# A transformer block on one core: the turned differences of the down weights pass through three buffers, the first square root goes first, and the order is another

## The chip, the cores and the metric

The kernel runs on one core of a Trainium2 chip. The metric is the device time of one execution in microseconds (us). Five engines work on it side by side, each through its own list of instructions in a fixed order: PE (TensorE, matrix products; PEld is its loading of weights), DVE (VectorE), ACT (ScalarE), POOL (GpSimd) and SP (SyncE, which here issues nearly all DMAs). An engine that reaches an instruction whose inputs aren't there yet waits, and everything behind that instruction in its list waits with it.

## The reference

One layer on 2048 rows of 640 numbers, in fp32: layer norm, windowed attention with 32 heads in which a row looks at 8 rows with a distance of 2 between them, a projection, a second layer norm, and a gated feed-forward part of width 1728.

```python
def _A_ref(x, wqkv, wo):                 # H = 32, Dh = 20, W = 8, dil = 2
    qkv = (x @ wqkv).reshape(B, S, 3, H, Dh)
    ...
    logits = jnp.einsum("bhsd,bhswd->bhsw", q, kg) * scale
    attn = _softmax(jnp.where(mask[None, None, :, :], logits, -1e9), axis=-1)
    o = jnp.einsum("bhsw,bhswd->bhsd", attn, vg)
    return o.transpose(0, 2, 1, 3).reshape(B, S, D) @ wo

def _B_ref(x, w_gate, w_up, w_down):
    return (_silu(x @ w_gate) * (x @ w_up)) @ w_down

h = x + _A_ref(_layernorm(x), A_wqkv, A_wo)
h2 = h + _B_ref(_layernorm(h), B_w_gate, B_w_up, B_w_down)
```

## The kernel before, in words

**Rows and numbers.** The 2048 rows are worked on in four blocks (0 to 3) of 512 rows, each as four groups of 128 rows. A product of two fp32 matrices is made of products of split numbers: each operand is cut into a high part (a cast to fp32r, on ACT) and the rest (a subtraction on DVE), and PE multiplies high by high, high by low and low by high. So ahead of most operands stand an ACT cast and a DVE subtraction.

**Stages.** First come the layer norms and the products with `wqkv` (L664), while DVE does the attention (L703 to L790) group by group up to about 564 us. The projection (`wo`, L911), the second layer norm and the feed-forward part follow block by block: `ffn(b)` for blocks 0 and 1 (L983, L994), and for blocks 2 and 3 a scheme in which products of sums and differences of the two blocks and of halves of the weights are combined. From that scheme come `early` (L1067, L1114), the ends of blocks 2 and 3 (L1089, L1124), `pair` (L1067 with L1208 to L1268) and `down_products` (L1315).

**The turned differences.** `down_combinations(p)`, for p = 0 to 5, loads two pieces of the down weights (L1141), makes four differences of them on DVE (L1144), and then twice, for h = 0 and 1: a copy to fp32r on ACT (L1147), the rest on DVE (L1148), and a store of both into the DRAM buffer `tsc` (L1150, 640 KB each). `down_products` reads them back at L1328. All twelve stores leave from one place of the tile `acts`, columns 2048 to 3328. A copy at L1147 therefore can't begin before the store ahead of it has read that place out.

**Start.** A dummy square root at L366 brings ACT's table of square roots in. The first 128 rows are loaded first (L593); `one_split` works on them on ACT (L442, a sum over columns 384 to 639) and on DVE (L446 to L450, the mean and its subtraction). Then come PE's transposes (L625), the casts (L627) and the rest (L628). Ten products of zeros (L575, `warm`) run on PE while the rows are on their way.

**What sets the order.** Every step is added to a planner `Plan` with its engine, a guessed cost, and what it reads and writes. The planner lists all 2846 steps by due times, and then moves single steps by a table `SHIFT` (step number: us) before it writes them out. `P.add` finds what a step must wait for from its reads and writes, so a new buffer gives other waits by itself.

**Names.** `fa` and `ra` are the large fp32 and fp32r tiles, `bank` is a PSUM bank, `lsc`, `msc`, `asc`, `osc` and `tsc` are buffers in DRAM. L1104 moves a finished product of `early` from its bank (ACT), L1007 and L1013 take the feed-forward product further on DVE, L1222 casts for `pair` on ACT.

Of the kernel before, what the change touches and what calls it, by code (L numbers as in the profile page):

```python
# [235 lines left out]
def dve(n):  # L236
    return 0.155 + 0.00104 * n
# [9 lines left out]
def act(n):  # L247
    return 0.185 + 0.00084 * n


def program(tc, x_in, wqkv_in, wo_in, ffn_in, ffl_in, const_in, out):
# [7 lines left out]
    with tc.tile_pool(name="sb", bufs=1) as sb, tc.tile_pool(  # L259
# [86 lines left out]
        def f(o, n):  # L346
            return fa[:, o : o + n]

        def rf(o, n):
            return ("fa", o, o + n)  # L350
# [1187 lines left out]
```

## Time and profile before

| | us |
|---|---|
| median of three runs | 842.88 (842.32 to 843.62) |
| the profiled execution, its own time | 843.94 |
| its span, first to last instruction | 842.1 |
| PE busy | 828.3 |
| DVE busy | 754.7 |
| ACT busy | 425.3 |

The span is what the trace shows; the 1.84 us between it and the execution's own time lie around it. Rows of a timeline give the start in us, the duration in us, engine, source line, operation, what is written and read, and in brackets how long the engine sat idle before and what ended that. Merged rows (x10) are several instructions on end. L numbers are lines of the kernel before.

### The profile page before, as it was taken

The numbers are of one execution on the slowest core, as the hardware profiler recorded it, in microseconds if no ns is written. First come the engines' busy times: TensorE is split into PE (matmuls) and PEld (weight loads), VectorE is DVE, ScalarE is ACT, GpSimd is POOL, SyncE is SP. The second block draws the span as 40 slices with busy tenths as digits, with TensorE's granted clock in tenths as the row PEclk, the third lists the DMA queues.
The fourth block names the chain that finished last, engine by engine and source line by source line (L and its number), as shares of the span: only waits on it lengthen the run. The fifth ranks groups of instructions, "written<-read, shape, count | busy, mean of one in ns | idle before, by whom it ended". The sixth has DMA issues, their size and how long they took to land.

```text
span 842.1 us, 11291 instructions
## 1 busy us (share of the span) xinstructions
PE 828.3 (98%) x4061; PEld 713.9 (85%) x4061; DVE 754.7 (90%) x916; ACT 425.3 (51%) x742; POOL 25.5 (3%) x34
## 2 busy tenths in 40 slices
PE   8999999999999999999999999999999999999997
PEld 6888888889988888888888988879878788888997
DVE  7599999999999999999999999987676997878982
ACT  7857474244673435745344376644684423233440
POOL 0000000000101000101000000000000000000000
PEclk9999999999999999999999999999999999999999
DMA  8896877559588685789799956999998643346722
GB/s 273 295 340 240 272 236 270 178 195 350 174 276 316 201 295 189 267 267 367 260 301 339 376 183 224 290 294 338 325 315 328 224 161 118 114 138 244 284 75 96
DMA packets 113223, 211.08 MB, mean 251 GB/s; under 512 B 37952, under 2 KB 70400, under 8 KB 112528
## 3 DMA queue, kind: packets, MB, share of 16 engines
q1 hardware_dynamic: 113008, 210.12, 72.5%
q8 instruction: 32, 0.52, 0.2%
q10 hardware_dynamic: 160, 0.25, 0.1%
q14 instruction: 23, 0.19, 0.1%
HBM read 151.27 MB, written 59.05 MB: 250 GB/s over the span
## 4 chain that ended last, share of the span: by engine, by line
PE 92%; DMA 4%; ACT 2%; DVE 1%; issue 0%; ACTq 0%
PE bank L664 25%; PE bank L983 22%; PE bank L1067 16%; PE bank L994 11%; PE bank L1315 7%; PE bank L911 7%; DMA tsc<-acts 3%; PE bank L1089 2%; PE bank L1124 1%; DMA ra<-lsc 1%; PE bank L1114 1%; DMA msc<-fa 1%; ACT acts L1147 0%; PE bank L625 0%; DVE acts L1148 0%
## 5 line engine op out<-in xcount | busy, mean ns | idle before, releaser
L983 PE MATMUL bank<-shb,ra 128*128 128x512 f32 x810 | 189.9, 390 | 0.7 <-ACT shb L527 0.7
L983 PEld LDWEIGHTS bank<-shb,ra 128*128 128x128 f32 x810 | 151.5, 188 | 31.9 <-ACT shb L527 1.0
L664 PE MATMUL bank<-ra,sha 128*128 128x480 f32 x480 | 105.9, 381 | 0.0
L664 PE MATMUL bank<-ra,shb 128*128 128x480 f32 x470 | 102.5, 378 | 0.0
L664 PEld LDWEIGHTS bank<-ra,sha 128*128 128x128 f32 x480 | 90.5, 189 | 13.8 <-ACT ra L638 0.3
L664 PEld LDWEIGHTS bank<-ra,shb 128*128 128x128 f32 x470 | 88.1, 188 | 13.2
L1067 PE MATMUL bank<-shb,ra 128*128 128x512 f32 x360 | 89.8, 395 | 3.2 <-DMA ra<-lsc 1.6
L748 DVE TENSOR_TENSOR fa<-fa 128x2560 f32<-128x2560 f32 x32 | 90.3, 2821 | 0.7
L713 DVE TENSOR_TENSOR fa<-fa 128x2560 f32<-128x2560 f32 x32 | 90.2, 2818 | 0.7 <-DMA fa<-qsc 0.4
L720 DVE TENSOR_REDUCE fa<-fa 128x128 f32<-128x2560 f32 x32 | 90.0, 2812 | 0.3
L1067 PEld LDWEIGHTS bank<-shb,ra 128*128 128x128 f32 x360 | 66.0, 188 | 19.4 <-ACT fa L1104 2.9
L994 PE MATMUL bank<-ra,acts 128*128 128x512 f32 x328 | 80.7, 390 | 0.0
L756 DVE TENSOR_TENSOR fa<-fa 128x1280 f32<-128x1280 f32 (+2 forms) x70 | 76.6, 1094 | 1.1
L911 PE MATMUL bank<-ra 128*128 128x320 f32 x480 | 74.0, 309 | 0.0
L911 PEld LDWEIGHTS bank<-ra 128*128 128x128 f32 x480 | 71.8, 188 | 2.2 <-ACT fa L914 0.8
L994 PEld LDWEIGHTS bank<-ra,acts 128*128 128x128 f32 x328 | 61.2, 188 | 12.5 <-DVE acts L1013 0.2
L669 ACT ACTIVATE st<-bank,fa 128x480 f32<-128x480 f32 x64 | 40.7, 658 | 59.9 <-PE bank L664 52.8
L1067 PE MATMUL bank<-ra 128*128 128x512 f32 x288 | 69.6, 391 | 1.3 <-ACT ra L1222 1.3
L1067 PEld LDWEIGHTS bank<-ra 128*128 128x128 f32 x288 | 53.7, 188 | 13.0 <-ACT ra L1222 1.7
L960 ACT CAST ra<-fa 128x1280 fp32r<-128x1280 f32 (+1 forms) x38 | 45.8, 1205 | 21.0 <-PE bank L983 9.0
L1240 DVE TENSOR_TENSOR fa<-bank,fa 128x512 f32<-128x512 f32 x60 | 40.9, 688 | 16.8 <-PE bank L1067 16.0
L1017 ACT CAST acts<-fa 128x512 fp32r<-128x512 f32 x34 | 21.1, 620 | 46.1 <-DVE fa L1007 46.0
(189 smaller groups left out, 1069.8 us busy)
## 6 DMA issues: line engine op xcount, KB each, us to landing
fa<-in_ffn_dram SPq DMA_DIRECT2D x28, 960.0 KB, 6.8
fa<-ksc SPq DMA_DIRECT2D x16, 880.0 KB, 6.7
fa<-vsc SPq DMA_DIRECT2D x16, 880.0 KB, 7.2
ra<-lsc SPq DMA_DIRECT2D x21, 640.0 KB, 6.6
ra<-lsc SPq DMA_DIRECT2D x27, 320.0 KB, 3.9
lsc<-ra SPq DMA_DIRECT2D x13, 640.0 KB, 4.5
tsc<-acts SPq DMA_DIRECT2D x12, 640.0 KB, 4.7
fa<-in_ffn_dram SPq DMA_DIRECT2D x12, 640.0 KB, 3.9
```

The costliest lines, as they stand in the source:

```text
L664: T.matmul(banks[bk][:, 0:480], l, r_(wq(g, w, c), 480), start=(p, c) == first_mm, stop=(p, c) == last_mm)
L713: P.add("DVE", dve(2560), lambda: V.tensor_tensor(f(PROD, 2560).rearrange("p (j w c) -> p j w c", j=2, w=W), window(ko, 2 * jp), f(qo + 32 ...
L720: P.add("DVE", dve(2560), lambda: V.tensor_reduce(f(lo + 128 * jp, 128), f(PROD, 2560).rearrange("p (n d) -> p n d", d=DH), axis=AX.X, op= ...
L748: V.tensor_tensor(f(PROD, 2560).rearrange("p (j w d) -> p j w d", j=2, d=DH), bass.AP(tensor=fa[:, vo : vo + 160].tensor, offset=fa[:, vo ...
L756: V.tensor_add(dst(v), v[:, :, 0:m, :], v[:, :, m : 2 * m, :])
L911: T.matmul(banks[bk][:, 0:320], l, r_(m, 320), start=p == 0 and c == 0, stop=p == 2 and c == NC - 1)
L960: P.add("ACT", act(n), lambda: A.copy(r_(gu, n), f(raw, n)), r=[rf(raw, n)], w=[rr(gu, n)], prio=PR["fh"])
L983: T.matmul(banks[bk], r_(gu + 1280 * w + wid * c + col, 128), x2(a, c), start=p == 0 and c == 0, stop=p == 2 and c == NC - 1)
L994: T.matmul(banks[bk][:, lo:hi], l, m, start=first and p == 0, stop=last and p == len(passes) - 1)
L1067: T.matmul(banks[bk], r_(ws[w] + 256 * q, 128), x(a, c), start=start and p == n == q == 0, stop=stop and p == 2 and n == len(terms) - 1 an ...
L1240: dv(0, lambda: V.tensor_add(fb(h, dst), banks[bk], fb(h, src)), [pb(bk)] + fr(h, src), fr(h, dst))
L1315: T.matmul(banks[bks[j]][:, 0:320], t(a, 128, 128 * j), r_(ws[w], 320), start=p == q == 0, stop=p == NP - 1 and q == 2)
```

## The change

There are three parts.

First, `one_split` reads the cell that the dummy square root writes. The step at L442 thus can't be put ahead of the square root at L366.

Second, the twelve turned pieces go in turn through three places: columns 2048 to 3328 of `acts` as before, and two places of 1280 columns in the upper half of `sha`, where block 1's rows lie until they are stored to the output. The first write there, which is the step for p = 0, h = 1, waits for the four stores of block 1's rows.

Third, `SHIFT` is another table, 318 entries in place of 508, so instructions stand in another order on all engines. The number of instructions of each kind is as before but for ACT's table loads, of which there are 32 in place of 34. The source lines from L443 to L1145 read 20 less after the change, L1147 is L1131, L1148 is L1132, L1150 is L1134, and the lines behind are 16 less.

```diff
 SHIFT = {
-    7: 4.3, 9: -21.9, 10: 1.5, 31: -334.6, 32: -146.2, 33: -164, 34: -58.2, 36: -482.1, 37: -247.2, 38: -3.6,
...
+    7: 3.5, 9: -106.8, 22: 0.4, 31: -515.8, 32: -221.5, 33: -238.8, 34: -84.5, 35: -34.6, 36: -483.8, 37:
...
             def one_split(self, j, cut=384):
                 src, xo = self.src(j), XN + 640 * j
                 P.add("ACT", 0.6, lambda: A.activation(f(xo + cut, 640 - cut), src[:, cut:640], AF.Identity, accum_out=f(self.SUM + j, 1)),
-                      r=[self.srcr(j), ("xh", 0, 2)], w=[rf(xo + cut, 640 - cut), rf(self.SUM + j, 1)], prio=self.prio)
+                      r=[self.srcr(j), ("xh", 0, 2), rf(LN + 119, 1)], w=[rf(xo + cut, 640 - cut), rf(self.SUM + j, 1)], prio=self.prio)
...
             for h in range(2):
-                o, src = 2048, t + 640 * h
-                P.add("ACT", act(640), lambda o=o, src=src: A.copy(act_t()[:, o : o + 640], f(src, 640)), r=rx(src, 640), w=[("ab", o, o + 640)], prio=PR["tp"])
-                P.add("DVE", dve(640), lambda o=o, src=src: V.tensor_sub(act_t()[:, o + 640 : o + 1280], f(src, 640), act_t()[:, o : o + 640].bitcast(F32)),
-                      r=rx(src, 640) + [("ab", o, o + 640)], w=[("ab", o + 640, o + 1280)], prio=PR["tp"])
-                P.add("SP", 0.45, lambda h=h, o=o: Q.dma_start(tsc[h, :, 1280 * p : 1280 * p + 1280], act_t()[:, o : o + 1280].bitcast(F32)),
-                    r=[("ab", o, o + 1280)], w=[(f"tq{h}", p, p + 1)], prio=PR["tp"], nbytes=nb(128, 5120))
+                src, n = t + 640 * h, (2 * p + h) % 3
+                o = 2048 if n == 0 else 1280 * (n - 1)
+                v = lambda a, m=640, o=o, n=n: (upper("turns", F32R) if n else act_t())[:, o + a : o + a + m]
+                key = lambda a, m=640, o=o, n=n: ("sha", 2560 + o + a, 2560 + o + a + m) if n else ("ab", o + a, o + a + m)
+                first = [("sha", 2560, 5120)] if p == 0 and h else [key(0)]
+                P.add("ACT", act(640), lambda v=v, src=src: A.copy(v(0), f(src, 640)), r=rx(src, 640), w=first, prio=PR["tp"])
+                P.add("DVE", dve(640), lambda v=v, src=src: V.tensor_sub(v(640), f(src, 640), v(0).bitcast(F32)),
+                      r=rx(src, 640) + [key(0)], w=[key(640)], prio=PR["tp"])
+                P.add("SP", 0.45, lambda h=h, v=v: Q.dma_start(tsc[h, :, 1280 * p : 1280 * p + 1280], v(0, 1280).bitcast(F32)),
+                    r=[key(0, 1280)], w=[(f"tq{h}", p, p + 1)], prio=PR["tp"], nbytes=nb(128, 5120))
```

Where the order is told below, a row is the place in the engine's list, the source line, the operation, what is written and read, and the shape; x2 is twice on end.

The first place is ACT's list at the start, before.

```order
2 L442 ACT_TABLE_LOAD
3 L442 ACTIVATE fa<-fa 128x256
4 L366 ACT_TABLE_LOAD
5 L366 ACTIVATE fa<-fa 128x1
6 L627 CAST sha_128<-bank_75 128x128
7 L627 CAST sha_128<-bank_74 128x512
8 L410 ACTIVATE fa<-fa 128x640
```

ACT's list at the start, after (L346 is L366 before, L422 is L442, L432 is L452, L607 is L627).

```order
2 L346 ACT_TABLE_LOAD
3 L346 ACTIVATE fa<-fa 128x1
4 L422 ACTIVATE fa<-fa 128x256
5 L432 ACTIVATE fa<-fa 128x640
6 L607 CAST sha_128<-bank_75 128x128
7 L607 CAST sha_128<-bank_74 128x512
8 L390 ACTIVATE fa<-fa 128x640
```

One table load stands ahead of the first rows' step instead of one ahead of it and one behind it, and a square of the first rows (L432) has come in between that step and the casts.

The second place is ACT's list, before, from the eighth to the tenth turned piece (L1147), which is from 626 to 641 us in the trace.

```order
523 L1147 CAST acts<-fa 128x640
524 L1168 CAST ra<-fa 128x1024
525 L1104 COPY fa<-bank_73 128x512
526 L1017 CAST acts<-fa 128x512
527 L960 CAST ra<-fa 128x1280
528 L1147 CAST acts<-fa 128x640
529 L1104 COPY fa<-bank_74 128x512
530 L1006 ACTIVATE fa<-bank_73 128x512
531 L960 CAST ra<-fa 128x1280
532 L1017 CAST acts<-fa 128x512
533 L1104 COPY fa<-bank_73 128x512
534 L1147 CAST acts<-fa 128x640
```

The same place on ACT, after, from the tenth to the twelfth piece (L1131 is L1147 before, L1084 is L1104, L1152 is L1168, L997 is L1017, L940 is L960, L986 is L1006).

```order
512 L1131 CAST acts<-fa 128x640
513 L940 CAST ra<-fa 128x1280
514 L1152 CAST ra<-fa 128x1024
515 L997 CAST acts<-fa 128x512
516 L1084 COPY fa<-bank_73 128x512
517 L1131 CAST turns<-fa 128x640
518 L1084 COPY fa<-bank_74 128x512
519 L1131 CAST turns<-fa 128x640
520 L986 ACTIVATE fa<-bank_73 128x512
521 L940 CAST ra<-fa 128x1280
522 L997 CAST acts<-fa 128x512
523 L1084 COPY fa<-bank_73 128x512
```

A turned piece still stands in front of the move of bank 74 (row 529 before, 518 after), but it is the eleventh of the twelve and no longer the ninth, and it writes to `turns`, as the twelfth does.

DVE at the same place, before: the list from the L1007 at 629.59 us on.

```order
602 L1007 TENSOR_TENSOR fa<-bank_74,fa 128x512
603 L1018 TENSOR_TENSOR acts<-fa,acts 128x512
604 L1144 TENSOR_TENSOR fa<-fa 128x320
605 L1148 TENSOR_TENSOR acts<-fa,acts 128x640
606 L1144 TENSOR_TENSOR fa<-fa 128x320 x2
607 L1007 TENSOR_TENSOR fa<-bank_74,fa 128x512
608 L1018 TENSOR_TENSOR acts<-fa,acts 128x512
609 L1148 TENSOR_TENSOR acts<-fa,acts 128x640
```

DVE from the same L1007 on, after (L987 is L1007 before, L998 is L1018, L1124 is L1144, L1132 is L1148; L1156 to L1161 are L1172 to L1177).

```order
595 L987 TENSOR_TENSOR fa<-bank_74,fa 128x512
596 L1124 TENSOR_TENSOR fa<-fa 128x320 x3
597 L998 TENSOR_TENSOR acts<-fa,acts 128x512
598 L1156 TENSOR_TENSOR fa<-fa,shb 128x1024
599 L1132 TENSOR_TENSOR turns<-fa,turns 128x640
600 L1159 TENSOR_TENSOR fa<-shb,fa 128x1024
601 L1132 TENSOR_TENSOR turns<-fa,turns 128x640
602 L1157 TENSOR_TENSOR fa<-fa,shb 128x1024
603 L1161 TENSOR_TENSOR fa<-shb,fa 128x1024
604 L987 TENSOR_TENSOR fa<-bank_74,fa 128x512
```

More work stands between the two steps that take a bank over (L1007 before, L987 after). From this first one up to the L1013 that PE's first L1124 waits for (L993 after, row 632 in both lists), thirteen instructions have come in (four of L1169, three of L1224, three of L1135, one each of L1221, L1240 and L1180) and four have gone out (two of L1144, two of L1148).

The third place is PE's list around that first L1124, at 662 us, before.

```order
503 L1114 MATMUL bank_71<-ra,acts 128x320 x3
504 L1089 MATMUL bank_74<-ra 128x512 x10
505 L1089 MATMUL bank_73<-ra 128x512 x15
506 L1067 MATMUL bank_74<-ra 128x512 x9
507 L1124 MATMUL bank_72<-ra,acts 128x320 x5
508 L1067 MATMUL bank_75<-ra 128x512 x4
```

PE's list around the same L1124, which is L1104 after (L1094 is L1114, L1069 is L1089, L1047 is L1067).

```order
499 L1094 MATMUL bank_71<-ra,acts 128x320 x3
500 L1069 MATMUL bank_74<-ra 128x512 x15
501 L1069 MATMUL bank_73<-ra 128x512 x15
502 L1047 MATMUL bank_74<-ra 128x512 x6
503 L1047 MATMUL bank_75<-ra 128x512 x6
504 L1047 MATMUL bank_74<-ra 128x512 x3
505 L1047 MATMUL bank_73<-ra 128x512 x6
506 L1047 MATMUL bank_75<-shb,ra 128x512 x4
507 L1104 MATMUL bank_72<-ra,acts 128x320 x5
```

Twenty-five products of L1067 stand ahead of it where there were nine.

88 rows, old and new, of the table SHIFT are left out of this document.

## The prediction

> **What bounds the kernel now.** I read first the page's busy times and its chain that ended last, then a table of stages, then PE's timeline for what is left idle.
>
> ```profile
> PE 828.3 (98%) x4061; PEld 713.9 (85%) x4061; DVE 754.7 (90%) x916; ACT 425.3 (51%) x742; POOL 25.5 (3%) x34
> PE 92%; DMA 4%; ACT 2%; DVE 1%; issue 0%; ACTq 0%
> ```
>
> PE is the bound: busy for 828.3 of 842.1 us, and 92% of the chain. The change takes no matmul away, so only PE's 13.8 idle us can be won, and new idle time on PE is lost in full. By stages (stretch; length; busy us of PE, PEld, DVE, ACT, POOL; granted clock; DMA share; GB/s):
>
> ```profile
> 0.00:14.00 14.00, 10.68 (x35) 7.78 (x36) 9.42 (x23) 9.66 (x21) 1.16 (x7) 0.89 0.75 248
> 20.00:238.00 218.00, 218.00 (x1050) 191.62 (x1049) 205.42 (x191) 119.35 (x237) 9.04 (x10) 1.00 0.77 259
> 238.00:556.00 318.00, 317.27 (x1491) 267.38 (x1490) 314.17 (x323) 168.13 (x259) 15.18 (x16) 1.00 0.79 275
> 556.00:683.00 127.00, 121.85 (x637) 104.89 (x636) 98.03 (x167) 71.30 (x121) 0.10 (x1) 1.00 0.83 288
> 683.00:836.20 153.20, 153.20 (x822) 136.01 (x821) 120.21 (x197) 50.96 (x88) 0.00 (x0) 1.00 0.46 159
> 836.20:842.10 5.90, 1.25 (x9) 0.99 (x7) 1.78 (x4) 0.00 (x0) 0.00 (x0) 0.85 0.30 111
> ```
>
> Idle us of PE: 3.32 at the start, none from 20 to 238, 0.73 up to 556, 5.15 up to 683, none up to 836.2, 4.65 in the tail, which keeps its shape in the new order. So the start and the stretch 556 to 683 can gain. PE's rows with idle time there:
>
> ```profile
> 6.30 1.21 PE L625 MATMUL bank<-fa 128*128 128x128 f32 x4 [0.36 <-DVE fa L450]
> 9.08 0.66 PE L625 MATMUL bank<-fa 128*128 128x128 f32 x4 [1.40 <-DVE sha L628]
> 567.23 0.96 PE L1067 MATMUL bank<-shb,ra 128*128 128x512 f32 x3 [1.57 <-DMA ra<-lsc]
> 610.09 0.97 PE L1067 MATMUL bank<-shb,ra 128*128 128x512 f32 x3 [0.49 <-ACT fa L1104]
> 613.87 0.66 PE L560 MATMUL bank<-fa 128*128 128x128 f32 x4 [0.61 <-ACT fa L1414]
> 635.87 1.43 PE L1067 MATMUL bank<-shb,ra 128*128 128x512 f32 x5 [1.08 <-ACT fa L1104]
> 660.08 1.20 PE L1067 MATMUL bank<-ra 128*128 128x512 f32 x4 [1.32 <-ACT ra L1222]
> ```
>
> The last five rows hold 5.07 of the 5.15 us. The sums are made on the profiled execution (843.94); the median of the runs, 842.88, is 1.06 lower, and from it I subtract the gains.
>
> **The change part by part: the start.** ACT, DVE and PE there, and the granted clock just behind:
>
> ```profile
> 3.79 1.28 ACT L442 ACT_TABLE_LOAD   x1 [3.79 <-DMA fa<-in_x_dram]
> 5.08 0.42 ACT L442 ACTIVATE fa<-fa 128x256 f32<-128x256 f32 x1
> 5.61 1.28 ACT L366 ACT_TABLE_LOAD   x1
> 5.62 0.21 DVE L447 TENSOR_SCALAR fa<-fa 128x1 f32<-128x1 f32 x1 [1.26 <-ACT fa L442]
> 3.60 2.34 PE L575 MATMUL bank<-ra 128*128 128x512 f32 x5
> 7.71 0.58 ACT L627 CAST sha<-bank 128x512 fp32r<-128x512 f32 x1 [0.46 <-PE bank L625]
> 10.00:14.40 4.40, 4.18 (x16) 3.53 (x17) 4.09 (x9) 4.40 (x13) 0.00 (x0) 0.61 0.82 281
> ```
>
> L442's table load waits for the rows to land (3.79), so the sum over them begins 1.28 us late; the second load (5.61) stands in front of the casts. The square root that now goes first reads a cell which DVE sets at the start, so its load lies in ACT's 3.79 idle us and costs nothing; were that cover gone, it would cost 1.28 as now. L442 and DVE's L447 come 1.28 us earlier. PE can't use all of that: its warm-up products end at 5.94 (3.60 + 2.34), so the transposes begin at about 5.95 in place of 6.30, which wins 0.36. The square of the first rows (L452 before) now stands in front of the casts; with ACT free 1.3 us earlier I take it to fit, and a little of the second wait (1.40) goes too. I take 0.6 in all; the bounds are 0, if the square holds the casts up, and 0.36 + 1.40 = 1.8.
>
> Behind that, 4.40 us ran at a mean clock of 0.61, which costs 4.40 x 0.39 = 1.7 us. I leave that as it is. [...]
>
> [...]
>
> **The load at 567.23.** It is issued only when PE has done with its place (an L1089). The new order puts two more products of L994 between that L1089 and the product that waits. PE's spacing of products is seen in a piece of the chain, 7.09 / 30 = 0.236 us:
>
> ```profile
> 635.87 7.09 PE bank L1067 x30
> ```
>
> I take 2 x 0.236 = 0.47 of gain; the bounds are 0 and the whole 1.57.
>
> **The three buffers.** Two groups of waits, two pieces of the chain, and ACT's rows behind them:
>
> ```profile
> ACT acts L1147 <- DMA tsc<-acts: 7.2, 7, 2.5
> DVE acts L1148 <- ACT acts L1147: 11.0, 8, 3.3
> 607.85 4.68 DMA tsc<-acts
> 612.61 0.72 ACT L1147 CAST acts<-fa 128x640 fp32r<-128x640 f32 x1 [0.46 <-DMA tsc<-acts]
> 613.24 0.58 ACT L1414 COPY fa<-bank 128x512 f32<-128x512 f32 x1
> 628.04 6.49 DMA tsc<-acts
> 634.61 0.72 ACT L1147 CAST acts<-fa 128x640 fp32r<-128x640 f32 x1 [2.51 <-DMA tsc<-acts]
> 635.24 0.58 ACT L1104 COPY fa<-bank 128x512 f32<-128x512 f32 x1
> ```
>
> Here a wait off PE reaches PE: the copy at 634.61 waits 2.51 us until the store issued at 628.04 has landed, L1104 stands behind it in ACT's list, and PE waits for L1104 (1.08). At 612.61 the same goes by way of L1414 (0.61). With three places a copy waits for the store three pieces back. These two stores, three pieces apart, were issued 20.2 us apart and landed after 4.68 and 6.49, so the wait has room to vanish, and 1.08 + 0.61 = 1.69 us of PE with it; the bounds are 0 and 1.69. The new wait, of the first write in the upper half for the four stores of block 1's rows, holds ACT's list (next in it L914 and L828 of block 3's projection); these stores now stand on SP ahead of the loads for the first piece, so they are under way before that piece exists, and I cost it at nothing. If that cover is gone, what is late is ACT by one landing, some 5 us.
>
> The other two waits, 0.49 and 1.32 = 1.81, are ACT and DVE being late with other work. The new order puts the casts of L1222 and their inputs (L1221) ahead of the last L1007 and the L1011, and block 3's projection earlier, so I take them off too; the bounds are 0 and 1.81.
>
> What is late next is DVE: other work is drawn into the room that its waits left. From the L1007 at 629.59 to the L1013 that PE's first L1124 waits for (start 661.59) thirteen instructions come in and four go out:
>
> ```profile
> 629.59:661.59 32.00, 29.60 (x142) 24.65 (x142) 24.77 (x34) 17.14 (x27) 0.00 (x0) 1.00 0.89 320
> L1169 DVE TENSOR_TENSOR shb<-fa,shb 128x1024 fp32r<-128x1024 f32 (+1 forms) x3 | 3.1, 1041 | 0.0
> L1224 DVE TENSOR_TENSOR ra<-fa,ra 128x512 fp32r<-128x512 f32 x24 | 16.3, 683 | 0.1
> L1135 DVE TENSOR_TENSOR fa<-bank,fa 128x640 f32<-128x640 f32 x12 | 9.4, 815 | 2.9 <-PE bank L1315 2.9
> L1148 DVE TENSOR_TENSOR acts<-fa,acts 128x640 fp32r<-128x640 f32 x12 | 9.9, 824 | 11.2 <-ACT acts L1147 11.0
> 630.96 0.69 DVE L1018 TENSOR_TENSOR acts<-fa,acts 128x512 fp32r<-128x512 f32 x1 [0.69 <-ACT acts L1017]
> ```
>
> In come four of L1169 (1.04 each), three of L1135 (0.815), and six of 512 columns, priced like L1224 (0.683): 10.7 us. Out go two of L1148 (0.824) and two of L1144, of half their width (0.5, estimate): 2.6. DVE thus has 24.8 + 8.1 = 32.9 us of work there. The time it has is 32.0, less the two waits of PE that go (2.4), plus sixteen products more ahead of that L1124 (25 for 9, 3.8 us), plus the six products by which the first L1007's bank is ready sooner (1.4): 34.8. The cushion is 1.9 us, and every us that DVE waits beyond it is a us of PE. I expect 0.7 of waiting at an L1018 as in the row, and 0.9 at the next two L1007, whose banks come about that late when I lay these durations out in the new lists. That is 1.6 and no loss; if one of the two turned pieces in there waits the mean (11.0 / 8 = 1.4) for its copy, 1.1 us are lost. I take 0.7, nearer to the latter; the bounds are 0 and what the last rival gives.
>
> From 20 to 556 PE's products keep nearly the same order and no row there has idle time to give but 0.73; I cost these stretches at nothing. What hides DVE's 314.17 busy us of 318 is that PE has other blocks' products to do; if DVE fell back there, the load at 567.23 would not be the thing PE waits for next, but block 3's projection.
>
> Sum: 0.6 + 0.47 + 1.69 + 1.81 - 0.7 = 3.87 us less. The profiled execution would be 840.1, the median 842.88 - 3.87 = 839.0.
>
> **The rivals.** *The waits only change places.* The 0.49 came from ACT's list alone, and ACT has the same work still, with the square roots and casts of block 3's layer norm set further forward, ahead of moves like L1104. If 556 to 683 keeps 3.5 us of such idle time, only start and load are won: 842.88 - 1.07 = 841.8. Against it: ACT is busy for 71.30 of the 127 us there.
>
> *The half clock at the start goes or moves.* With 1.7 us more won it is 837.3. [...]
>
> *Slower: DVE becomes the bound between 629 and 663.* If both turned pieces in that stretch wait the longest of before (3.3) and three L1018 wait 0.69 each, with the 0.9 that is 9.6 us of waiting, 7.7 beyond the cushion: 4.57 of gains less 7.7 is 3.1 more, 846.0. It is slower than before from 6.5 us of waiting on (1.9 + 4.57) and by over 0.2% from 8.2 on. For it: DVE's work there goes from 24.8 to 32.9 us, 99% of it once the waits are gone. Against it: with three places the copies come early.
>
> *The buffers do nothing*, as the first write stands in ACT's list until the four stores have landed, 5 us: that takes away the 1.69 and more, and ends near the first rival, in whose chance it is.
>
> **How the numbers follow.** About 0.2% (1.7 us) is what a measurement of this kernel can tell from no change. Forecast 0.55, its own range 837.2 (start as taken, the other bounds of gain: 0.6 + 1.57 + 3.5 = 5.67 less) to 841.0 (nothing at the start, 0.47, and half of the middle's 2.8). Waits change places 0.18, from 841.0 to 843.0, of which 0.07 is faster by over 0.2% and 0.11 the same. Half clock gone 0.10. DVE bound 0.17, of which 0.13 is slower by over 0.2% and 0.04 the same. Faster 0.55 + 0.07 + 0.10 = 0.72, same 0.15, slower 0.13. The range 836.9 to 843.8 leaves out half of the clock's case (0.05) and most of the DVE's (0.12).
>
> **What would show it.** In the changed profile: one table load on ACT before 3.8 us and PE's first transposes at 5.95 (start); no wait of ACT at L1131 for a `tsc` store, and no 5 us wait at its second copy (buffers); PE idle between 556 and 683 of 1.5 to 2 us in place of 5.15, of which about 1.1 is the load; DVE busy for over 90% from 627 to 660. The forecast is wrong if PE waits over 3 us for DVE rows there (L987, L993), or if idle time shows up in 20 to 556 or 683 to 836, where I expect none.

## The result, and the profile after

The changed kernel takes 837.75 us (median of six runs, 835.97 to 839.46), the kernel before in the same session 843.25 (six runs, 842.05 to 844.50). The ratio is 0.9936, with a 95% interval of 0.9919 to 0.9952: 0.64% faster, 5.4 us. Run again beside other kernels it gave 0.9933 (0.9916 to 0.9951). The forecast was 839.0, with a range of 836.9 to 843.8. The profiled execution took 839.46 (span 837.3), 4.5 less than the profiled one of before. One run in this document, of the kernel with three places alone, took 912.27 us at a granted clock of 0.85; it is in that kernel's median and not in its ratio.

The page's busy times and its chain, after:

```profile
PE 827.1 (99%) x4061; PEld 713.5 (85%) x4061; DVE 756.1 (90%) x916; ACT 421.0 (50%) x740; POOL 23.1 (3%) x34
PE 86%; DVE 7%; DMA 3%; issue 2%; ACT 0%; SPq 0%; DVEq 0%; ACTq 0%
```

PE is idle for 10.2 us in place of 13.8, and DVE now holds 7% of the chain where it held 1%. By stages, in the columns of the prediction's table:

```profile
0.00:14.00 14.00, 10.88 (x41) 8.65 (x42) 10.38 (x26) 9.77 (x24) 1.16 (x7) 0.88 0.80 258
238.00:556.00 318.00, 316.74 (x1482) 266.24 (x1481) 312.48 (x318) 165.13 (x256) 12.75 (x16) 1.00 0.82 280
556.00:683.00 127.00, 125.54 (x651) 108.06 (x649) 106.48 (x178) 71.02 (x123) 0.00 (x0) 1.00 0.84 287
627.00:660.00 33.00, 33.00 (x158) 27.71 (x157) 30.91 (x41) 18.99 (x30) 0.00 (x0) 1.00 0.83 284
```

From 556 to 683 PE is idle for 1.46 us where it was 5.15, and DVE is busy for 8.5 us more: work from later has moved in. From 627 to 660 PE has no idle time and DVE is busy 94% of the time. PE's rows with idle time, after:

```profile
8.30 1.11 PE L605 MATMUL bank<-fa 128*128 128x128 f32 x4 [1.77 <-DVE sha L608]
239.38 13.90 PE L963 MATMUL bank<-shb,ra 128*128 128x512 f32 x60 [1.22 <-DVE shb L508]
566.27 1.65 PE L1047 MATMUL bank<-shb,ra 128*128 128x512 f32 x6 [0.57 <-DVE fa L991]
577.53 8.62 PE L891 MATMUL bank<-ra 128*128 128x320 f32 x57 [0.58 <-ACT ra L808]
595.95 4.66 PE L891 MATMUL bank<-ra 128*128 128x320 f32 x30 [0.15 <-ACT fa L894]
607.12 2.12 PE L1047 MATMUL bank<-shb,ra 128*128 128x512 f32 x8 [0.15 <-ACT fa L986]
```

All four waits of before from 610 to 660 us are gone, and so is the one for the `lsc` load. What the buffers were to do shows in the groups of waits, after:

```profile
ACT acts L1131 <- DMA tsc<-acts: 2.4, 1, 2.4
DVE acts L1132 <- ACT acts L1131: 2.2, 2, 1.2
```

ACT waited for a `tsc` store 7 times for 7.2 us; now once for 2.4, and no row of PE waits for it (a second profile of the changed kernel, told of below, has none). DVE's waits behind the copies went from 11.0 to 2.2 us. The start on ACT and PE, after:

```profile
1.34 1.28 ACT L346 ACT_TABLE_LOAD   x1 [1.34 <-PEq L1511]
4.22 0.42 ACT L422 ACTIVATE fa<-fa 128x256 f32<-128x256 f32 x1 [1.39 <-DMA fa<-in_x_dram]
5.57 0.96 PE L605 MATMUL bank<-fa 128*128 128x128 f32 x5
```

The table is loaded from 1.34 to 2.62, under the wait for the rows, and PE's first transposes begin at 5.57 instead of 6.30, though the rows landed 0.43 later (4.22, before 3.79); in the second profile they begin at 5.74. Where both lists of PE have the same products behind them, the next product starts earlier after the change by 1.5 us at 16 us, 1.0 at 239, 0.4 at 559, 0.25 at 588, 1.5 at 623, 2.9 at 633 and 4.3 at 656. In this execution, then, nearly all that the start and the load had won was lost again by 588, and what is left was won from 610 to 656. In the second profile the figures are 2.3 at 15, 1.6 at 558, 2.25 at 586 and 7.1 at 653, with a granted clock of 1.00 from 8 to 16 us, where this execution has 0.79.

### The profile page after: what moved, and what is told of

Same layout as the page of the kernel before. It is cut to its first block, busy times and chain, and to the rows that moved or that the text cites. A ratio compares the mean times of both kernels' runs of the same rounds, so it can differ in the third digit from the quotient of the medians.

```text
span 837.3 us, 11299 instructions
## 1 busy us (share of the span) xinstructions
PE 827.1 (99%) x4061; PEld 713.5 (85%) x4061; DVE 756.1 (90%) x916; ACT 421.0 (50%) x740; POOL 23.1 (3%) x34
## 4 chain that ended last, share of the span: by engine, by line
PE 86%; DVE 7%; DMA 3%; issue 2%; ACT 0%; SPq 0%; DVEq 0%; ACTq 0%
PE bank L963 22%; PE bank L644 20%; PE bank L1047 16%; PE bank L974 11%; PE bank L1299 7%; PE bank L891 4%; PE bank L1069 2%; DVE fa L693 1%; DVE fa L700 1%; DMA tsc<-acts 1%; DMA ra<-lsc 1%; PE bank L1094 1%; DVE fa L736 1%; PE bank L1104 1%; DMA fa<-in_ffn_dram 1%
## 5 line engine op out<-in xcount | busy, mean ns | idle before, releaser
L1047 PE MATMUL bank<-shb,ra 128*128 128x512 f32 x360 | 89.7, 395 | 0.7 <-DVE fa L991 0.6
L1047 PEld LDWEIGHTS bank<-shb,ra 128*128 128x128 f32 x360 | 65.8, 188 | 16.8 <-DVE fa L1224 1.7
L1047 PE MATMUL bank<-ra 128*128 128x512 f32 x288 | 69.1, 390 | 0.0
L1047 PEld LDWEIGHTS bank<-ra 128*128 128x128 f32 x288 | 53.9, 188 | 11.2
L1224 DVE TENSOR_TENSOR fa<-bank,fa 128x512 f32<-128x512 f32 x60 | 41.1, 690 | 19.9 <-PE bank L1047 19.1
L940 ACT CAST ra<-fa 128x1280 fp32r<-128x1280 f32 (+1 forms) x38 | 45.6, 1206 | 24.2 <-PE bank L963 12.3
L997 ACT CAST acts<-fa 128x512 fp32r<-128x512 f32 x34 | 21.0, 619 | 47.6 <-DVE fa L987 45.9
```

The lines of the kernel that those rows point to most:

```text
L940: P.add("ACT", act(n), lambda: A.copy(r_(gu, n), f(raw, n)), r=[rf(raw, n)], w=[rr(gu, n)], prio=PR["fh"])
L1047: T.matmul(banks[bk], r_(ws[w] + 256 * q, 128), x(a, c), start=start and p == n == q == 0, stop=stop and p == 2 and n == len(terms) - 1 an ...
```

## The experiments

To take the parts apart the order was written out: `RANK` lists the 2846 steps in the order in which the kernel before, or the changed one, issues them, and a step goes out in that order as soon as all that it depends on is out. The two lists unchanged give the two kernels' own orders.

```diff
-        key = [(t + SHIFT.get(n, 0.0), n) for n, t in enumerate(start)]
-        heap, out = [key[n] for n in range(len(ops)) if not left[n]], []
+        at = {n: i for i, n in enumerate(RANK)}
+        heap, out = [at[n] for n in range(len(self.ops)) if not left[n]], []
...
-            n = heapq.heappop(heap)[1]
+            n = RANK[heapq.heappop(heap)]
```

Line numbers of these kernels are their own; where rows are quoted, the line of the kernel before is given.

**The square root first, alone, in the old order.** Step 2 is the square root, step 31 the first rows' step.

```diff
-                      r=[self.srcr(j), ("xh", 0, 2)], w=[rf(xo + cut, 640 - cut), rf(self.SUM + j, 1)], prio=self.prio)
+                      r=[self.srcr(j), ("xh", 0, 2), rf(LN + 119, 1)], w=[rf(xo + cut, 640 - cut), rf(self.SUM + j, 1)], prio=self.prio)
...
-    31, 32, 33, 34, 2,
+    2, 31, 32, 33, 34,
```

> The kernel before in its own order, with the square root ahead of the first rows' step and nothing else changed. If the parts add up, this one gives what PE won at the start of the changed kernel's trace, 0.5 to 1.5 us: 841.7 to 842.7 where before stands at 843.2. PE's first transposes begin at 5.6 to 6.0 instead of 6.30, ACT loads one table before the rows land, and the waits at 610, 614, 636 and 660 us stay as they were. If what was won at the start is only the half clock falling elsewhere, the time is within 0.4 us of before, and the stretch at half clock covers as many products as before.

Measured: 841.53 for 842.19 (12 and 27 runs), ratio 0.9995 (0.9987 to 1.0004), 0.4 us with an interval that holds zero. In its trace PE's first transposes begin at 5.74 and the second ones at 8.41, 0.67 earlier than before (9.08). The waits at 610, 614 and 660 us stayed, as expected (0.49, 0.80, 1.32); the one at 636 did not: it is 0.17, and no longer behind the `tsc` store but behind the next step of ACT, though this kernel has one place as before. The profiles also show why 0.4 is hard to see. The row of this kernel for 8 to 16 us, that of before and, from a later run, that of the changed kernel with the first rows' step first:

```profile
8.00:16.00 8.00, 7.34 (x39) 6.12 (x40) 7.75 (x18) 7.94 (x21) 0.00 (x0) 1.00 0.96 321
```

```profile
8.00:16.00 8.00, 6.67 (x29) 5.48 (x30) 7.51 (x18) 7.94 (x20) 0.00 (x0) 0.79 0.88 310
```

```profile
8.00:16.00 8.00, 6.65 (x25) 5.87 (x26) 7.51 (x18) 7.83 (x21) 0.00 (x0) 0.57 0.80 281
```

The granted clock over these 8 us is 1.00, 0.79 and 0.57, which is 0, 8 x 0.21 = 1.7 and 8 x 0.43 = 3.4 us of PE's time (an estimate, as if PE were busy throughout), larger than what is to be measured.

**Three places, alone, in the old order.** `down_combinations` as in the change; the fourth store of block 1's rows (step 1791) goes right behind the third (1789).

```diff
-                o, src = 2048, t + 640 * h
+                src, n = t + 640 * h, (2 * p + h) % 3
...
     1789,
+    1791,
...
-    1791,
```

> The kernel before in its own order, with three places for the turned differences and the fourth store of block 1's rows put right behind the third on SP; the square root stays where it was. If the tsc wait was the cause of two of PE's waits, ACT's wait for tsc stores falls from 7.2 us to under 1, PE's waits of 0.61 and 1.08 us go and those of 0.49 and 1.32 stay: 1.7 us less, 841.5. If the waits only change places without a new order, the time is within 0.5 us of before and PE waits as long for something else between 610 and 662.

Measured: 841.53 for 842.19 (11 and 27 runs), ratio 0.9987 (0.9977 to 0.9998), 1.1 us (0.2 to 1.9). ACT's waits for `tsc` stores are gone from its groups. PE's row at 635 us, and ACT's rows ahead of it (L1142 is L1147, L1095 is L1104, L997 is L1006):

```profile
634.72 2.56 PE L1058 MATMUL bank<-shb,ra 128*128 128x512 f32 x10 [0.78 <-ACT fa L997]
```

```profile
629.10 0.72 ACT L1142 CAST turns<-fa 128x640 fp32r<-128x640 f32 x1
629.73 0.58 ACT L1095 COPY fa<-bank 128x512 f32<-128x512 f32 x1
634.07 0.60 ACT L997 ACTIVATE fa<-bank 128x512 f32<-128x512 f32 x1 [3.76 <-DMA asc<-fa]
```

The copy comes 5.5 us earlier than in the trace before, and L1104 with it (PE is 1.0 us earlier at 566). But the next step of ACT waits for another store, `asc`, and PE for that: of 1.08 us only 0.30 are won. PE's waits of 0.49 and 0.61 at 610 and 614 are both gone, and one of 0.35 is new. So the expectation of 1.7 was too high, and its reason half right: the waits at 610 and 614 hung on the stores (they are gone in all four profiles with three places in the old order), the one at 636 had a second cause right behind the first (0.69 to 1.08 in these four). The 1.08 itself is no fixed size: with the square root alone, and one place, it was 0.17.

**Both, in the old order.** The two edits together.

> The two parts together, still in the order before. If they are independent the gains add: 2.2 to 3.2 us less than before, 840.0 to 841.0, and the new order accounts for the other 2.3 to 3.3 us of the change. If the new order is what makes the buffers pay, this is within 0.7 us of the kernel with the square root alone.

Measured: 839.70 for 842.19 (9 and 27 runs), ratio 0.9972 (0.9962 to 0.9982), 2.4 us; run again (below) 0.9971. The sum of the two single ones is 1.5, each of them with some 0.8 to either side, so that they add is neither shown nor excluded.

**The new order with one place.** The changed kernel, `down_combinations` as before, and the stores of the tenth and eleventh piece right behind their subtractions, since the new order has them 31 and 13 places later in SP's list than the old one.

```diff
-                src, n = t + 640 * h, (2 * p + h) % 3
+                o, src = 2048, t + 640 * h
...
     2055,
+    2056,
...
     2064,
+    2065,
...
-    2065,
...
-    2056,
```

> The changed kernel's order and start, with one place for the turned differences as before (each store right behind its subtraction where the new order had put it later). PE's list is that of the changed kernel. If the order leans on the buffers, each of the last copies waits 4 to 6 us for the store ahead, ACT waits over 15 us for tsc stores in all, moves to the banks stand behind it, and the time is 3 us or more above the changed kernel: 841 or more. If the order alone is what pays, it is within 1 us of the changed kernel, 837.0 to 838.8.

Measured: 881.60 for 842.19 (4 and 27 runs), ratio 1.0472 (1.0456 to 1.0489): 40 us slower than before, though PE's list is that of the changed kernel. Groups of waits, and two rows of ACT with the row behind each (L1138 is L1147, L905 is L914):

```profile
ACT acts L1138 <- DMA tsc<-acts: 46.6, 10, 8.7
DVE acts L1139 <- ACT acts L1138: 23.8, 7, 8.1
PE bank L902 <- ACT fa L905: 14.5, 2, 7.5
```

```profile
587.49 0.72 ACT L1138 CAST acts<-fa 128x640 fp32r<-128x640 f32 x1 [8.73 <-DMA tsc<-acts]
588.12 0.42 ACT L905 COPY fa<-bank 128x320 f32<-128x320 f32 x1
608.51 0.72 ACT L1138 CAST acts<-fa 128x640 fp32r<-128x640 f32 x1 [8.64 <-DMA tsc<-acts]
609.14 0.74 ACT L905 COPY fa<-bank 128x320 f32<-128x320 f32 x2
```

Two of the twelve copies, the sixth and seventh, stand 7 and 5 steps later in ACT's list than in the changed kernel's, as a copy goes out only behind the store ahead of it. The new order sets the copies close together (the second stands right behind the first), ahead of the moves of the projection's banks, and PE waits for these moves. The direction was expected, "3 us or more"; the size was not. PE's granted clock is part of it:

```profile
556.00:620.00 64.00, 48.60 (x261) 43.60 (x259) 39.38 (x76) 23.22 (x42) 0.00 (x0) 0.89 0.75 252
620.00:683.00 63.00, 45.45 (x191) 36.55 (x192) 31.87 (x50) 32.41 (x54) 0.00 (x0) 0.86 0.61 215
```

Besides 33 us of idle time, PE has a granted clock of 0.89 and 0.86 here, and 1.00 from 238 to 556. PE's longest waits here are 7.0 and 7.5 us; that they brought the clock down is not shown.

**The new order with two places.** One in `acts`, one in the upper half of `sha`; the two late stores moved as above.

```diff
-                src, n = t + 640 * h, (2 * p + h) % 3
+                src, n = t + 640 * h, (2 * p + h) % 2
```

> The changed kernel's order with two places for the turned differences (one in acts, one in the upper half of sha), and the stores of the tenth and eleventh piece right behind their subtraction. PE's list is that of the changed kernel. If the order needs a place to be free some 6 us after a store is issued, the third, sixth, eleventh and twelfth copy, which lie 2 to 9 us behind the store of the piece two back, wait 1.5 to 5 us each: ACT waits 10 to 14 us for tsc stores, and the time is 840 to 846. If two places are enough, ACT waits under 5 us and the time is within 1 us of the changed kernel.

Measured: 852.37 for 842.36 (5 and 23 runs), ratio 1.0121 (1.0100 to 1.0142). ACT's waits:

```profile
ACT turns L1142 <- DMA tsc<-turns: 8.7, 3, 5.9
ACT acts L1142 <- DMA tsc<-acts: 6.8, 2, 5.3
```

15.5 us in five waits, near to the expected 10 to 14; the time came out 6 us above the expected range's end. From 556 to 690 us PE is idle for 9.1 us where it was 1.5 in the changed kernel, and its granted clock is 0.96 there. Three places are no luxury in this order: it is slower than before with one and with two.

**The changed kernel without the square root first.**

```diff
-    2, 31,
+    31, 2,
```

> The changed kernel with the first rows' step ahead of the square root on ACT, as before the change; all else in its order. If the square root first is worth what it brought in the old order (0.4 us in the median, 0.7 us earlier transposes in the trace), this is 838.0 to 838.7. If the start bounds nothing, it is 837.7 as the changed kernel; if the new order leans on it (a square of the first rows now stands right behind, with another table load ahead of it), 839.5 or more.

Measured: 839.06 for 842.36 (12 and 23 runs), ratio 0.9960 (0.9944 to 0.9975), 3.4 us less than before, where the changed kernel has 5.4 to 5.6. In this order the square root first is thus worth 2.0 to 2.2 us by these ratios; put beside the 837.75 of the changed kernel that is about 839.9, in the expected case that the new order leans on it (839.5 or more). The intervals overlap, so its size stays loose. Its profile has PE's first transposes at 6.42, the second ones at 9.35 (8.30 and 8.41 in the two profiles of the changed kernel, 0.9 to 1.05 earlier), and the clock of 0.57 quoted above. Part of the 2 us may thus be the clock: over the whole run it is 0.996 in 4 of the 12 runs here, and 0.997 or more in all 12 of the changed kernel. Whether the clock from 8 to 16 us is low more often with this start, so few runs don't show.

**Two moves on DVE in the changed kernel.** The reduction at 238.30 (step 631) goes behind the steps that the product at 239.38 waits for, and two moves of banks (1830, 1832) behind the subtractions for the projection at 577.53.

```diff
-    631, 1017, 1022, 1015, 1005,
+    1017, 1022, 1015, 1005, 631,
...
-    1830, 2083, 1831, 2084, 2085, 1833, 2201, 1832, 2086, 2087,
+    2083, 1831, 2084, 2085, 1833, 2201, 2086, 2087, 1830, 1832,
```

> The changed kernel with two moves on DVE: the reduction of 32 columns at 238.30 us behind the two steps that PE's first feed-forward product waits for, and the two moves of banks at 576.26 and 577.00 behind the two subtractions that block 3's projection waits for. If these waits are DVE's order alone, PE's waits of 1.22 and 0.58 us become about 0.7 and 0.1: 0.9 us less than the changed kernel, 836.8. If DVE's time is what counts there, the same waits come back under another name and the time stays.

Measured: 838.12 for 842.36 (6 and 23 runs), ratio 0.9949 (0.9930 to 0.9968), and beside the changed kernel (below) the same as that. In its profile PE waits 0.7 at 240 us and not at all from there to the tail, and yet the time is no shorter.

**Order alone at 658 us.** The both-parts kernel, with one cast of L1222 moved ahead of L1010 and its inputs (L1179, L1221) ahead of the last turned piece.

```diff
-    2067, 2195, 2203, 2298, 2068, 2204, 2196, 2174, 2234,
+    2174, 2234, 2067, 2195, 2203, 2298, 2068, 2204, 2196,
...
-    2205, 2235,
+    2235, 2205,
```

> The kernel before in its order with square root first and three places (the third run of the first four), and with one of the two first casts for the pairs moved ahead of the last half-width activation on ACT, with its two inputs ahead of the last turned piece and the last rounding on DVE. If PE's wait of 1.32 us at 658 us is the order of these steps, it goes and the time is 1.2 us less than that run's, about 838.8 where before stands at 842.5. If it is DVE's amount of work, the wait moves to the half-width activation and the time is that run's, 840.

Measured: 840.26 for 842.36 (12 and 23 runs), ratio 0.9978 (0.9965 to 0.9990), no faster than without the move. PE's rows there (L1217 is L1222, L1219 is L1224):

```profile
654.67 1.66 PE L1058 MATMUL bank<-ra 128*128 128x512 f32 x6 [1.04 <-ACT ra L1217]
656.74 0.96 PE L1058 MATMUL bank<-ra 128*128 128x512 f32 x3 [0.41 <-DVE ra L1219]
```

1.45 us in two waits instead of 1.32 in one; the wait stayed at the casts and did not go to the half-width activation, as the second case had it. DVE's rows follow each other without a pause from 651.77 to 658.01 here, so putting one step in front of another doesn't help. What helps, as I read it, is to have had the work done earlier, which the changed kernel does: there the twelfth piece's subtraction stands at 632, and not at 656 as before. No run moved that alone, so this cause is argued and not shown.

**The changed kernel again, and beside it the two moves and the two parts.**

> The changed kernel again, its order written out as a list, to stand beside the next three on one chip. All theories: 0.992 to 0.995 of before.

> The changed kernel with the two moves on DVE again, beside it on one chip. The earlier profile had no wait of PE left between 241 us and the tail, against 1.3 us in the changed kernel's, and 0.74 for 1.22 at 240 us. If these waits are what counts, it is 1.0 to 1.8 us faster than the changed kernel; if PE loses the same in another form, within 0.4 us of it.

> Square root first and three places in the old order again, beside the changed kernel on one chip. If the three parts add up, it lies 2.5 to 3.5 us above the changed kernel; the difference is what the new order brings once the two other parts are there.

Measured, all with 842.76 for before (23 runs): the changed kernel 837.45 (6 runs), ratio 0.9933 (0.9916 to 0.9951); the two moves 837.81 (6 runs), 0.9934 (0.9917 to 0.9951); the two parts in the old order 840.11 (12 runs), 0.9971 (0.9959 to 0.9982). The new order is worth 2.7 to 3.2 us once the other two parts are there. The changed kernel's second profile has PE's waits of 0.73 at 238 and 0.53 at 565, and none of the 0.58, 0.15 and 0.15 of the first; the two moves' second profile has 0.7 and 0.55. So in that execution the two moves had nothing to gain.

**More work for DVE.** The changed kernel, with three subtractions of L1169 done twice, about 3.4 us.

```diff
         for n in order:
             P.ops[n][2]()
+            if n in (2165, 2169, 2179):
+                P.ops[n][2]()
```

> The changed kernel with three of DVE's subtractions of 1024 columns done twice (some 3.4 us more work for DVE between the two L987 at 640 and 650 us, the result is the same). If DVE's cushion there is about 1.9 us, as the prediction counts it, and 1.84 us of it is used up by the waits that the changed kernel's trace shows, PE waits for a step of DVE by 1.5 to 3.4 us before 663 us, and the time is that much more than the changed kernel's. If DVE is not near to bounding, PE waits under 0.5 us there and the time stays within 0.5 us.

Measured: 842.48 for 842.76 (12 and 23 runs), ratio 0.9990 (0.9975 to 1.0004), 5.0 us more than the changed kernel beside it. PE's rows, and DVE's ahead of the second (L1164 is L1169, L1009 is L1018):

```profile
645.57 0.56 PE L1105 MATMUL bank<-ra,acts 128*128 128x320 f32 x2 [0.62 <-ACT acts L1008]
648.17 1.00 PE L1105 MATMUL bank<-ra,acts 128*128 128x320 f32 x5 [2.05 <-DVE acts L1009]
```

```profile
645.03 2.49 DVE L1164 TENSOR_TENSOR shb<-fa,shb 128x1024 fp32r<-128x1024 f32 x2 [0.29 <-ACT shb L1163]
647.44 0.68 DVE L1009 TENSOR_TENSOR acts<-fa,acts 128x512 fp32r<-128x512 f32 x1
```

PE waits 2.67 us for 3.4 us of work, in the expected range. By the products' starts 3.0 us are lost between 640 and 655, and 0.65 at the start (clock 0.79 from 8 to 16 us in this one, 1.00 in the other), which about makes up the 3.5 by which the spans of the two profiles differ (838.0 and 834.5). The median's 5.0 holds something else besides: five of the twelve runs have a granted clock of 0.998 or more and take 840.4 to 840.7, about 3.1 above the changed kernel, whose six runs beside it all have such a clock; the other seven have 0.993 to 0.996 and take 842.4 to 844.4. Where those lose their clock no profile shows. So DVE was near to being the bound, and 3.4 us of its work cost about 3 us at like clock.

## Why the prediction was right, point by point

The direction and the likeliest case held: the forecast was 3.87 us, and 5.4 was measured. The waits didn't change places: from 556 to 683 PE was idle for 1.46 and 0.55 us in the two profiles, where that rival wanted 3.5. The terms:

*Start, 0.6.* The load of the table went under the wait for the rows, as said. Alone it measures 0.4 (-0.3 to 1.1), in the new order some 2.0, part of which may be clock. By the second transposes PE was 0.67 to 0.78 earlier, near to the 0.6. The split was not as told, though: nothing of the wait for L628 went, it is 1.77 and 1.40 in the two profiles where it was 1.40, and the gain came at the first transposes (0.73 and 0.56). Over 14 profiles of 11 kernels the clock from 8 to 16 us is 1.00 in five, 0.79 in eight and 0.57 in one, and the changed kernel itself has 0.79 in one and 1.00 in the other. So one order can have the half clock (0.50 from 9 to 11 us in the first of these two, from 11 to 14 in the trace of before) and not have it, and the rival "half clock goes" is in large part spread between runs; what brings that clock on, and that the order has no influence on how often, is not shown.

*The load at 567, 0.47.* Undersized in this pair of profiles. In place of 1.57 there is no wait for the load, and one of 0.57 right behind it for L1011 on DVE: 1.0 net. But the wait for the load was no fixed size: in six profiles of the old order it is between nothing and 2.15 us (mean 1.14), and in all eight of the new order it is gone, with 0 to 0.61 (mean 0.48) behind it, so about 0.7 net. The two products in between were counted rightly; not counted was SP. Its line in the chain before (issue and time to landing), and its row of issue after:

```profile
560.54 6.64 DMA ra<-lsc
```

```profile
559.13 2.12 SPq L945 DMA_DIRECT2D ra<-lsc  x1
```

After the change PE's product ends at 559.10 and the load is issued at once; before, PE was done at 559.99 and SP issued it only at 560.54, behind another load.

*The buffers, 1.69.* This term's split was wrong, as the run with three places alone shows: 0.61 went as said, and the 0.49 too, which I had put down to ACT's other work; of 1.08, 0.78 came back at the next step, behind an `asc` store. In all 1.1 us (0.2 to 1.9). The step that failed is "the wait has room to vanish, and 1.08 + 0.61 of PE with it": I hadn't asked what stands behind L1104 on ACT.

*The order, 1.81.* The two waits went, but only the 1.32 by the order (it is 1.32 to 1.45 in all profiles of the old order, and gone in the new). The move at 658 alone shows that reordering one of the casts, which is how I had it, doesn't do it; that DVE had the turned pieces done 24 us earlier, which needs the places, is the likely cause and is not shown by a run of its own. In sum the new order brought 2.7 to 3.2 us.

*New waits on DVE, -0.7.* PE had none between 627 and 660. The cushion agrees with the count, though: the stretch from that L987 (626.82) to L993 (660.89) took 34.07 us with DVE busy for 31.95, where 34.8 and 32.9 had been counted, 2.1 over for 1.9, and DVE waited 1.84 us there, in two rows:

```profile
643.78 0.69 DVE L1153 TENSOR_TENSOR shb<-fa,shb 128x512 fp32r<-128x512 f32 x1 [1.39 <-ACT shb L1152]
645.51 1.23 DVE L1153 TENSOR_TENSOR shb<-fa,shb 128x1024 fp32r<-128x1024 f32 x1 [0.45 <-ACT shb L1152]
```

The turned pieces waited little, and the waits came at other steps. 3.4 us more work gave PE 2.67 us of idle time, which is the slower rival's mechanism at work, about where it was put.

*The first write's wait for the four stores* cost nothing: the second copy ran at 581.38, right behind the first, and the last of the stores was issued at 573.6. *20 to 556* was costed at nothing, and idle time there had been named as a sign of being wrong. The gain did shrink there: in the profiled execution by 0.5 us at 239 and by another 0.5 up to 559, in pauses too short to have a row, most of it around 390; in the second profile by nothing at 239 and by 0.7 up to 558.

So the sum was right partly by luck: the buffers were oversized and the loss from 20 to 556 was left out, while the -0.7 for DVE never came and the start may have brought more than its term; these offset each other. The idle time of the row at 660.08 in the trace of before, 1.32, is also less than what that wait cost. Ahead of it a product starts at 658.38, the one behind it at 660.08 and the next 0.34 later, 2.04 us for two steps that take 0.47 elsewhere, so this wait cost about 1.6.

## What to carry to other kernels

Buffers and order are one change: three places in the old order brought 1.1 us, the new order with one place lost 40 and with two 10, and together with the square root they won 5.4. When a wait is taken from an engine's list, look at the next instruction there and what it waits for, before the whole of PE's wait is counted as won. Where a filler (here DVE at 94%) is drawn into the room that a wait leaves, count its work against the time up to the next step that PE needs; that cushion, counted here as 1.9 us with 1.84 of it used, is what the next change has to live on.

## What the runs showed that I had not expected

The cost of a place short was far larger than I had thought: with one place ACT waited 46.6 us for stores, ten times up to 8.7, and the kernel lost 40 us, part of it at a lower granted clock (0.89 and 0.86 from 556 to 683). And the spread of one kernel's runs, 839.94 to 844.56 over 27 runs of before, is nearly as wide as the gain; the clock from 8 to 16 us, 1.00 to 0.57 in the profiles, is worth 0 to 3.4 us by the estimate above, so a single pair of profiles would not have told 0.4 from 2 us. The same holds for single waits: the one for the load at 567 was between nothing and 2.15 us in six profiles of the old order, and the one at 636 was 1.08 in the profile of before and 0.17 in that of a kernel that differs from it at the start alone.
